# A fused attention and spectral-mix kernel: pairing other key blocks, and value products over 64 partitions

## The chip, the cores and the metric

The kernel runs on one core of a Trainium2 chip. The metric is the device time of one execution in microseconds, and the number to predict is the median of the changed kernel's runs. The kernel before takes 438.14 us (median of three runs, 438.12 to 438.55).

## The reference

The reference is a sliding-window attention whose output feeds a spectral layer. Batch, heads, sequence and head size are 8, 8, 576 and 64; a query sees itself and the 127 keys before it, with a linear bias by distance.

```python
scores = scale * np.matmul(q, k.transpose(0, 1, 3, 2))
rel = pos[:, None] - pos[None, :]
mask = (rel >= 0) & (rel < window)                  # window = 128
scores = np.where(mask, scores + bias[None], -1e9)  # bias = -slope(head) * |rel|
attn = np.exp(scores - max); attn = attn / attn.sum(-1)
x = np.matmul(attn, v)                              # 8 x 576 x 512 after the heads are joined
X = np.fft.rfft(x, axis=1)                          # the first 64 modes are kept
Yr = Xr @ w_r - Xi @ w_i ;  Yi = Xr @ w_i + Xi @ w_r   # per mode, 512 x 512 weights
u = x + np.fft.irfft(Y)
out = u + np.maximum(u @ w_ch, 0.0)
```

The weights `moe_w_r` and `moe_w_i` are 64 matrices of 512 x 512 in fp32 each, 134 MB together. They are by far the largest input; `q`, `k` and `v` are 9.4 MB each.

## The kernel before, in words

The kernel has two parts that overlap in their transfers. The **attention part** works through 16 units; a unit is one batch entry and four heads. A table `STAGE` (line 38) fixes by hand the order in which the steps of neighbouring units are issued, with a lag for each step; one pass through the table is called a stage here, and a stage finishes one unit's worth of each step. The **spectral part** streams the 128 weight matrices through TensorE (line 886) and ends with the projections and the output.

For a unit, `q` and `k` are loaded in fp32, cast to bf16 by VectorE (line 251), transposed by TensorE (line 263) and copied out by ScalarE (line 269), so that the head's 64 dimensions lie on partitions. `score` (line 274) multiplies keys by queries. The 576 tokens are four full blocks of 128 (numbers 0 to 3) and a tail of 64. A score tile holds two key blocks. A block has 128 keys, and they are taken as 64 pairs: the even keys (j = 0) and the odd keys (j = 1) of a block are the two halves of the free dimension, and the two blocks of a tile are the two halves of the partitions. So partitions 0 to 63 belong to the first block of the tile, partitions 64 to 127 to the second. In the kernel before, tile pair 0 holds blocks 0 and 1, pair 1 holds blocks 2 and 3. `exp` (line 305) runs on ScalarE; pair 0 is then multiplied by a table of decays on VectorE (`mask`, line 312), while pair 1 got its bias by a matmul with the identity (line 284) before the exponent.

`value` (line 320) multiplies the attention tile, as the stationary operand (128 partitions by 128 queries), by the values `vb`. Since the two halves of the partitions hold different key blocks, whose windows reach different query tiles, `vb` is laid out with zeros: the values of the first block fill columns 0 to 65 of its rows and zeros the rest, the values of the second block columns 66 to 131 (64 columns of values and two of ones, for the sum). One matmul of 132 columns over all 128 partitions thus serves two neighbouring query tiles. `vt` holds the tail keys. `norm` (line 352) divides by the sums on VectorE.

The values are loaded by five DMAs for each unit: one for each head, 128 partitions by two pieces of 512 bytes (line 212), and one for the tail, which writes partitions 64 to 95 (line 225). They go through the SP queue, which holds nothing else during attention but the loads of `q` and `k`. The last two units' values go through the POOL queue in three DMAs (lines 219 and 225), because their place in time is among POOL's weight loads. The cast of the values (line 246) takes two VectorE instructions of 64 partitions, one for each half, and line 248 casts the tail. After a cast, the loads for the unit after next are issued, so each kind of input has two buffers.

What sets the order of the weight loads: POOL issues them in program order. In most stages of the attention part, POOL first copies one element of the cast `k` of the unit after next (`gate`, line 565) and then issues one weight load of 512 KB (as bf16; the DMA reads 1 MB of fp32 and casts). From stage 12 on it also loads weights into the buffers of `q`, `k` and `v` that are no longer needed (line 472 with tiles `qr`, `kr`, `vr`), and then packs of two matrices into memory that the attention part gives back (line 491). POOL's own work at the start is the masks' distances (line 159) and the zeros and ones of `vb` and `vt` (lines 139 to 142).

Of the kernel before, what the change touches and what calls it, by code (L numbers as in the profile page):

```python
# [11 lines left out]
BF16 = mybir.dt.bfloat16  # L12
I32 = mybir.dt.int32
AF = mybir.ActivationFunctionType
ALU = mybir.AluOpType
# [5 lines left out]
P = 128  # L21
D = 64
# [5 lines left out]
FULL = 4  # L28
# [2 lines left out]
TPP = 9  # L31

W = D + 2

NC = 24

# [70 lines left out]
class _Attention:  # L107


    def __init__(self, tc, ctx, q, k, v, consts, x, XC, raw):  # L110
        self.tc, self.nc = tc, tc.nc
        self.q, self.k, self.v = q, k, v
        self.ident, self.F, self.FT = consts
        self.x, self.XC = x, XC
        B, H, S, _ = q.shape
        self.S, self.NG = S, H // 4
        self.units = [(b, g) for b in range(B) for g in range(self.NG)]
        self.raw = raw
        end = ctx.enter_context(tc.tile_pool(name="aend", bufs=1))
        self.sums = ctx.enter_context(tc.tile_pool(name="asum", bufs=2))  # L120
        self.mid = ctx.enter_context(tc.tile_pool(name="amid", bufs=2))
        self.ps = ctx.enter_context(tc.tile_pool(name="aps", bufs=1, space=PSUM))
        fix = ctx.enter_context(tc.tile_pool(name="afix", bufs=1))
        self.table = fix.tile([P, H, 2, 2 * P], BF16, name="mask")
        self.bias = fix.tile([P, H, 2, 2 * P], BF16, name="bias")
        self.qkT = [fix.tile([P, 2, 2, (FULL + 1) * P], BF16, name=f"qkT{i}") for i in range(2)]
        at = (fix, end)
        self.att = [at[i].tile([P, FULL * 8 * P + 64], BF16, name=f"att{i}") for i in range(2)]
        self.vb = [at[i].tile([P, 2, 4, 2, 2 * W], BF16, name=f"vb{i}") for i in range(2)]
        self.vt = [end.tile([P, 4, 2, W], BF16, name=f"vt{i}") for i in range(2)]  # L130
        self.loaded, self.casted, self.open = {}, {}, {}

    def fixtures(self, i):
        nc = self.nc
        for t, tail in ((self.vb[i], self.vt[i]),):
            for half in range(2):
                row = slice(64 * half, 64 * half + 64)
                c0 = W * half
                nc.gpsimd.memset(t[row, :, :, :, W - c0 : 2 * W - c0], 0.0)
                nc.gpsimd.memset(t[row, :, :, :, c0 + D : c0 + W], 1.0)  # L140
            nc.gpsimd.memset(tail, 0.0)
            nc.gpsimd.memset(tail[64:96, :, :, D:], 1.0)
        nc.gpsimd.memset(self.att[i][:, FULL * 8 * P :], 1.0)

    def distances(self, pool):

        nc = self.nc
        key_i = pool.tile([P, 2, 2], I32)
        for half in range(2):
            nc.gpsimd.iota(key_i[64 * half : 64 * half + 64], [[1, 2], [-P, 2]], base=0,  # L150
                           channel_multiplier=2)
        key = pool.tile([P, 2, 2], FP32)
        nc.gpsimd.tensor_copy(key, key_i)
        self.near = [pool.tile([P, 2, 2 * P], BF16) for _ in range(2)]

        def window(out, half, c0, width, n):
            row = slice(64 * half, 64 * half + 64)
            sign = 1 - 2 * n
            nc.gpsimd.affine_select(
                out=out[row, :, c0 : c0 + width],  # L160
                in_=key[row, :, n].unsqueeze(-1).broadcast_to([64, 2, width]),
                compare_op=ALU.is_ge, fill=-float(2**20), base=-n,
                pattern=[[-sign, 2], [sign, width]], channel_multiplier=-2 * sign,
            )

        for half in range(2):
            for n in range(2):
                window(self.near[0], half, n * P, P, n)
        nc.gpsimd.tensor_copy(self.near[1][:64], self.near[0][:64])
        nc.gpsimd.tensor_copy(self.near[1][64:, :, : P + TAIL], self.near[0][64:, :, : P + TAIL])  # L170
        window(self.near[1], 1, P + TAIL, TAIL, 0)

    def slope(self, h):
        return 2.0 ** (-8.0 * (h + 1) / self.table.shape[1])
# [26 lines left out]
    def load(self, w, u):  # L201
# [5 lines left out]
        if w == "v":  # L207
            t = self.raw[w][:, u % 2]
            sv = self.v[b, hs]
            if u < len(self.units) - 2:  # L210
                for h in range(4):
                    nc.sync.dma_start(
                        out=t[:, :2, h],
                        in_=sv[h, : FULL * P].rearrange("(r p j) d -> p r (j d)", r=2, j=2),
                    )
                queue = nc.sync
            else:
                for r in range(2):
                    nc.gpsimd.dma_start(
                        out=t[:, r],  # L220
                        in_=sv[:, 2 * r * P : 2 * (r + 1) * P].rearrange(
                            "h (p j) d -> p h (j d)", j=2),
                    )
                queue = nc.gpsimd
            queue.dma_start(
                out=t[64:96, 2],
                in_=sv[:, FULL * P :].rearrange("h (p j) d -> p h (j d)", j=2),
            )
        else:
            t = self.raw[w][:, u % 2]  # L230
            src = (self.q, self.k)["qk".index(w)][b, hs]
            nc.sync.dma_start(
                out=t.rearrange("p e j d -> p e (j d)"),
                in_=src.rearrange("(e h) (p j) d -> (h p) e (j d)", h=2, j=TPP),
            )
        self.loaded[w, u] = t

    def cast(self, u, w):
# [2 lines left out]
        src = self.loaded.pop((w, u))  # L241
        if w == "v":
            src = src.rearrange("p s h (j d) -> p s h j d", j=2)
            for half in range(2):
                row = slice(64 * half, 64 * half + 64)
                nc.vector.tensor_copy(  # L246
                    self.vb[u % 2][row, :, :, :, W * half : W * half + D], src[row, :2])
            nc.vector.tensor_copy(self.vt[u % 2][64:96, :, :, :D], src[64:96, 2])
        else:
            dst = self.mid.tile([P, TPP, 2, D], BF16, tag=w, name=w)  # L250
# [23 lines left out]
    def score(self, u, t):  # L274
# [12 lines left out]
                )  # L287
        for j in range(2):
            for half in range(2):
                blk = 2 * pair + half  # L290
                spans = [(blk * P, 0, min(2 * P, self.S - blk * P))]
                if blk == FULL - 1:
                    spans.append((FULL * P, 192, TAIL))
                for k0, c0, n in spans:
                    for e in range(2):
                        row = slice(64 * e, 64 * e + 64)
                        nc.tensor.matmul(  # L297
                            sc[64 * half : 64 * half + 64, e, j * 256 + c0 : j * 256 + c0 + n],
                            lhsT=qkT[row, 1, h, k0 + j : k0 + P : 2],
                            rhs=qkT[row, 0, h, k0 : k0 + n],  # L300
                            start=not biased, stop=True, skip_group_check=biased,
                        )
        self.open[t, u] = sc
# [16 lines left out]
    def value(self, u, e):  # L320
# [1 line left out]

        nc = self.nc
        b, g = self.units[u]
        odd = b % 2
        att, vb, vt = self.att[u % 2], self.vb[u % 2], self.vt[u % 2]
        last = u == len(self.units) - 1 and e == 1
        av = self.ps.tile([P, 2, 512], FP32, tag="sc" if last else "av", bufs=2 if last else 1)
        for h in range(2):
            bank = av[:, h, : (FULL + 1) * W]  # L330
            todo = []
            for pair in range(2):
                rhs = [vb[:, pair, 2 * e + h, j] for j in range(2)]
                todo.append((pair, 0, 2 * pair, rhs))
                if pair == 1 and odd:
                    todo.append((pair, P, 3, [r[:, :W] for r in rhs]))
                    todo.append((pair, P - 64, 4, [r[:, W:] for r in rhs]))
                else:
                    todo.append((pair, P, 2 * pair + 1, rhs))
            todo.append((1, 192 - 64 * odd, 4, [vt[:, 2 * e + h, j] for j in range(2)]))  # L340
            for n, (pair, c0, qt, rhs) in enumerate(todo):
                for j in range(2):
                    o = (((2 * pair + h) * 2 + e) * 2 + j) * 256 + c0
                    nc.tensor.matmul(  # L344
                        bank[:, qt * W : qt * W + rhs[j].shape[1]],
                        lhsT=att[:, o : o + P], rhs=rhs[j],
                        start=(n == 0 and j == 0), stop=(n == len(todo) - 1 and j == 1),
                        skip_group_check=True,
                    )
        self.open["av", e, u] = av  # L350

    def norm(self, u, e):
# [2 lines left out]
        av = self.open.pop(("av", e, u))  # L355
        cs = slice((4 * g + 2 * e) * D, (4 * g + 2 * e + 2) * D)
        rec = self.sums.tile([P, 2, FULL + 1], FP32, tag="rec", name="rec")
        tiles = av[:, :, : (FULL + 1) * W].rearrange("p h (t n) -> p h t n", n=W)
        nc.vector.reciprocal(rec, tiles[:, :, :, D])
        nc.vector.tensor_tensor(  # L360
            out=self.x[:, b, :, cs].rearrange("p t (h d) -> p h t d", h=2),
# [667 lines left out]
```

## Time and profile before

| | before |
|---|---|
| median of three runs | 438.14 us |
| profiled execution | 437.99 us |
| its span | 436.1 us |
| busy share of the span: PE, DVE, ACT, POOL | 73%, 42%, 37%, 21% |
| read from HBM, written | 162.5 MB, 9.4 MB |
| granted TensorE clock, mean of the span | 0.862 |

All shares and times below the first two rows are of the profiled execution. Its span is 1.89 us shorter than its time; this remainder lies around the span. A line such as `2.00:8.00` of the windows gives the busy time of each engine in that stretch, then the granted clock, the mean busy share of the 16 DMA engines (packets of one engine overlap, so it can exceed 1) and the bytes that arrived, in GB/s. Weights count there in bf16, though twice as many bytes are read.

### The profile page before, as it was taken

How to read it: one execution, taken by the hardware profiler on the slowest of the kernel's cores; microseconds unless marked ns; L12 is line 12 of the kernel's file. 1: busy time of each engine (PE TensorE's matmuls, PEld its weight loads, DVE VectorE, ACT ScalarE, POOL GpSimd, SP SyncE). 2: the span in 40 equal slices, each digit the busy share in tenths (PEclk: the TensorE clock that was granted, in tenths of full speed). 3: DMA queues.
4: the chain of work that ended last, by engine and by line, in shares of the span. 5: the costliest groups of instructions: out<-in, count | busy, mean ns of one | idle time of the engine just before them, and what ended most of it. 6: DMA issues, size and time to landing. Idle time of an engine off the chain costs nothing.

```text
span 436.1 us, 8292 instructions
## 1 busy us (share of the span) xinstructions
PE 316.2 (73%) x3488; PEld 177.7 (41%) x3509; DVE 184.5 (42%) x332; ACT 162.3 (37%) x211; POOL 90.2 (21%) x170
## 2 busy tenths in 40 slices
PE   5589899979686635543442487999889999788982
PEld 4367677757565312111111133444434444334430
DVE  7789799887783301000000021322213233122684
ACT  6949899988681000000000011322222322102780
POOL 8701010103424002222112110101111110012600
PEclk9969999999999955555555569999999999989997
DMA  8999999999999999999999999999999999998598
GB/s 285 326 311 310 290 316 300 307 298 299 252 217 212 215 215 213 214 214 214 215 212 214 214 215 214 215 214 215 215 214 214 215 215 215 213 215 153 190 378 311
DMA packets 50453, 105.54 MB, mean 242 GB/s; under 512 B 4032, under 2 KB 21072, under 8 KB 50416
## 3 DMA queue, kind: packets, MB, share of 16 engines
q0 software_dynamic: 19440, 68.41, 77.9%
q1 hardware_dynamic: 30976, 36.60, 25.3%
q8 instruction: 27, 0.44, 0.4%
q14 instruction: 10, 0.08, 0.1%
HBM read 162.53 MB, written 9.44 MB: 394 GB/s over the span
## 4 chain that ended last, share of the span: by engine, by line
DMA 71%; PE 10%; DVE 8%; issue 5%; POOL 2%; ACT 1%; SPq 1%; DVEq 0%; POOLq 0%; ACTq 0%
DMA w<-in_moe_w_i_dram 42%; DMA wch<-in_moe_w_ch_dram 8%; DMA qr<-in_q_dram 7%; DMA vr<-in_v_dram 6%; DVE o L842 3%; DMA qr<-in_moe_w_i_dram 3%; PE my L702 2%; DMA vr<-in_moe_w_r_dram 2%; DMA kr<-in_k_dram 2%; DVE vb L246 1%; PE acc L886 1%; PE av L344 1%; POOL Z L648 1%; PE my L659 1%; DVE att L318 1%
## 5 line engine op out<-in xcount | busy, mean ns | idle before, releaser
L886 PE MATMUL acc<-w,XC 128*32 128x512 bf16 x456 | 80.3, 478 | 68.5 <-DMA w<-in_moe_w_i_dram 34.2
L886 PEld LDWEIGHTS <-XC 128*32 128x32 bf16 x508 | 38.4, 147 | 109.2 <-issue 82.8
L307 ACT ACTIVATE att<-sc 128x1024 bf16<-128x1024 f32 x64 | 64.1, 1032 | 9.7 <-PE sc L297 9.6
L636 ACT CAST ZW<-zw 128x512 bf16<-128x512 f32 x8 | 4.7, 585 | 142.9 <-PE zw L634 142.9
L344 PE MATMUL av<-vb,att 128*128 128x132 bf16 (+1 forms) x576 | 38.4, 217 | 13.3 <-DVE x L360 8.6
L344 PEld LDWEIGHTS <-att 128*128 128x128 bf16 x704 | 36.6, 98 | 18.7 <-DVE x L360 12.0
L608 DVE TENSOR_SCALAR yq<-acc 128x512 bf16<-128x512 f32 x14 | 9.6, 687 | 81.8 <-PE acc L886 81.8
L702 PE MATMUL my<-wch,xT 128*64 128x512 bf16 x288 | 34.5, 381 | 5.7 <-ACT x L733 4.2
L711 ACT CAST XW<-my 128x512 bf16<-128x512 f32 x36 | 19.3, 589 | 50.5 <-PE my L659 50.5
L683 DVE COPY xT<-tr 128x1024 bf16<-128x1024 bf16 x18 | 12.4, 692 | 54.9 <-PE tr L681 54.9
L269 ACT COPY qkT<-tp 128x1152 bf16<-128x1152 bf16 x30 | 33.5, 1116 | 4.1 <-PE tp L263 3.6
L491 POOL DMA_DIRECT2D w<-in_moe_w_r_dram x22 | 15.6, 710 | 72.1 <-PE acc L886 46.1
L491 POOL DMA_DIRECT2D w<-in_moe_w_i_dram x23 | 16.3, 709 | 64.1 <-PE acc L886 45.3
L297 PE MATMUL sc<-qkT 64*64 64x256 bf16 (+2 forms) x640 | 25.1, 263 | 4.8 <-ACT qkT L269 1.2
L360 DVE TENSOR_TENSOR x<-av,rec 128x640 bf16<-128x640 f32 x32 | 26.4, 825 | 1.1
L702 PEld LDWEIGHTS <-xT 128*64 128x64 bf16 x288 | 17.1, 109 | 21.5 <-issue 9.1
L246 DVE CAST vb<-vr 64x1024 bf16<-64x1024 f32 x32 | 22.6, 708 | 0.2
L733 ACT CAST x<-my 128x512 bf16<-128x512 f32 x18 | 10.5, 585 | 31.6 <-PE my L659 31.6
L297 PEld LDWEIGHTS <-qkT 64*64 64x64 bf16 x640 | 14.5, 109 | 19.1 <-issue 16.0
L734 DVE CAST x<-my 128x512 bf16<-128x512 f32 x18 | 12.4, 692 | 21.7 <-PE my L659 21.7
L842 DVE TENSOR_TENSOR o<-yy,r 128x1024 f32<-128x1024 f32 (+1 forms) x20 | 20.3, 1059 | 2.1 <-ACT r L802 1.9
L318 DVE TENSOR_TENSOR att<-att,mask 128x1024 bf16<-128x1024 bf16 x32 | 20.5, 682 | 0.0
(137 smaller groups left out, 424.7 us busy)
## 6 DMA issues: line engine op xcount, KB each, us to landing
w<-in_moe_w_i_dram POOLq DMA_DIRECT2D x23, 1024.0 KB, 36.2
w<-in_moe_w_r_dram POOLq DMA_DIRECT2D x22, 1024.0 KB, 35.6
qr<-in_q_dram SPq DMA_DIRECT2D x16, 576.0 KB, 7.9
kr<-in_k_dram SPq DMA_DIRECT2D x16, 576.0 KB, 7.9
w<-in_moe_w_r_dram POOLq DMA_DIRECT2D x16, 512.0 KB, 14.2
vr<-in_v_dram SPq DMA_DIRECT2D x56, 128.0 KB, 7.6
w<-in_moe_w_i_dram POOLq DMA_DIRECT2D x13, 512.0 KB, 24.0
out_dram<-o SPq DMA_DIRECT2D x13, 512.0 KB, 5.0
```

The lines of the kernel that those rows point to most:

```text
L246: nc.vector.tensor_copy(self.vb[u % 2][row, :, :, :, W * half : W * half + D], src[row, :2])
L269: (self.nc.vector.tensor_copy if u < 2 and w == "q" else self.nc.scalar.copy)(dst.rearrange("q h (p j) -> q h p j", j=TPP), tp.rearrange(" ...
L297: nc.tensor.matmul(sc[64 * half : 64 * half + 64, e, j * 256 + c0 : j * 256 + c0 + n], lhsT=qkT[row, 1, h, k0 + j : k0 + P : 2], rhs=qkT[r ...
L307: self.nc.scalar.activation(self.att[u % 2][:, kt * 8 * P : (kt + 1) * 8 * P], sc.rearrange("p e n -> p (e n)"), AF.Exp, scale=1.0 / math. ...
L318: nc.vector.tensor_tensor(out=rows, in0=rows, in1=self.table[:, heads], op=ALU.mult)
L344: nc.tensor.matmul(bank[:, qt * W : qt * W + rhs[j].shape[1]], lhsT=att[:, o : o + P], rhs=rhs[j], start=(n == 0 and j == 0), stop=(n == l ...
L360: nc.vector.tensor_tensor(out=self.x[:, b, :, cs].rearrange("p t (h d) -> p h t d", h=2), in0=tiles[:, :, :, :D], in1=rec.unsqueeze(-1).br ...
L491: nc.gpsimd.dma_start(out=t.rearrange("p s a e -> p s (a e)"), in_=w[kinds.pop()][m : m + 2].rearrange("m (p a) e -> p m (a e)", a=4))
L702: nc.tensor.matmul(mm[ROWS[half]], lhsT=lhsT, rhs=wch[:, dt], start=(dt == 0), stop=False, skip_group_check=True,)
L711: nc.scalar.copy(XW[:, j, n], mms[n])
L842: nc.vector.tensor_tensor(out=o[:, c], in0=yy[:, c], in1=r[:, c], op=ALU.add)
L886: nc.tensor.matmul(into[32 * (m % 4) : 32 * (m % 4) + 32], lhsT=XC[:, c0 : c0 + 31 * NM + 1 : NM], rhs=wq[t][a], start=(ri == 0 and a == 0 ...
```

## The change

The tile pairs become blocks 1 and 2, and blocks 0 and 3 (`BLOCKS`). In pair 0, the first half's queries are tiles 1 and 2; the second half (block 2) covers query tiles 2 and 3, and its columns are placed so that query tile 2 lies in the same columns for both halves. For one of the two key parities this needs the span to be cut in two. So query tile 2 is the one that both halves of a pair share, and its product still contracts over 128 partitions. All other products take one half: 64 partitions of attention weights by 64 partitions of values, 66 columns wide. `vb` loses its zeros and is half as wide. One VectorE instruction of 128 partitions casts it. The output tile `av` is laid out by query tile in steps of `SLOT`, with both heads side by side, so query tiles 0 to 2 lie in one PSUM bank and 3 and 4 in the next. `value` issues the products of the lower half and of the upper half in turn, two heads each, and the shared tile and the tail keys at the end: 32 matmuls where there were 20 (even batch entries) or 24 (odd).

The values are still loaded by five DMAs for each unit, but the block order changes what each writes: two DMAs of two heads for blocks 1 and 2 (128 partitions), one of four heads for block 0 (partitions 0 to 63), one of four heads for block 3 (partitions 64 to 127), and the tail. Every contiguous piece is 512 bytes, as before. The last two units use the same five on the POOL queue instead of three. On POOL, the memsets of the zeros go, and the distances take more and smaller selects.

```diff
+SLOT = 172
+BLOCKS = ((1, 2), (0, 3))
...
-        self.vb = [at[i].tile([P, 2, 4, 2, 2 * W], BF16, name=f"vb{i}") for i in range(2)]
+        self.vb = [at[i].tile([P, 2, 4, 2, W], BF16, name=f"vb{i}") for i in range(2)]
...
-                nc.gpsimd.memset(t[row, :, :, :, W - c0 : 2 * W - c0], 0.0)
-                nc.gpsimd.memset(t[row, :, :, :, c0 + D : c0 + W], 1.0)
...
+        nc.gpsimd.memset(self.vb[i][:, :, :, :, D:], 1.0)
...
-            if u < len(self.units) - 2:
-                for h in range(4):
-                    nc.sync.dma_start(
-                        out=t[:, :2, h],
-                        in_=sv[h, : FULL * P].rearrange("(r p j) d -> p r (j d)", r=2, j=2),
...
-                for r in range(2):
-                    nc.gpsimd.dma_start(
-                        out=t[:, r],
...
+            queue = nc.sync if u < len(self.units) - 2 else nc.gpsimd
+            for rows, r, first in ((slice(0, P), 0, 1), (slice(0, 64), 1, 0), (slice(64, P), 1, 3)):
+                for hh in (slice(0, 2), slice(2, 4)) if r == 0 else (slice(0, 4),):
+                    n = 2 * (rows.stop - rows.start)
+                    queue.dma_start(
+                        out=t[rows, r, hh],
+                        in_=sv[hh, first * P : first * P + n].rearrange("h (p j) d -> p h (j d)", j=2),
...
-            for half in range(2):
-                row = slice(64 * half, 64 * half + 64)
-                nc.vector.tensor_copy(
-                    self.vb[u % 2][row, :, :, :, W * half : W * half + D], src[row, :2])
+            nc.vector.tensor_copy(self.vb[u % 2][:, :, :, :, :D], src[:, :2])
...
-                blk = 2 * pair + half
-                spans = [(blk * P, 0, min(2 * P, self.S - blk * P))]
-                if blk == FULL - 1:
-                    spans.append((FULL * P, 192, TAIL))
...
+                k0, c0 = BLOCKS[pair][half] * P, 2 * P * j
+                spans = [(k0, k0, c0, min(2 * P, self.S - k0))]
+                if biased and half:
+                    spans.append((FULL * P, FULL * P, c0 + 3 * TAIL, TAIL))
+                elif half and j == 0:
+                    spans = [(k0, k0, P, 2 * P)]
+                elif half:
+                    spans = [(k0, k0, 3 * P, P), (k0, k0 + P, 0, P)]
...
+        for j in range(2):
+            c0 = 2 * P * j
+            todo += [(low, 1, 0, c0, vb, j), (high, 0, 3, 2 * P - c0, vb, j),
+                     (low, 1, 1, c0 + P, vb, j), (high, 1, 3, c0, vb, j),
+                     (low, 0, 1, c0, vb, j), (high, 1, 4, c0 + P - back, vb, j)]
+            far += [(slice(0, P), 0, 2, c0 + P, vb, j), (high, 1, 4, c0 + 3 * TAIL - back, vt, j)]
+        started = set()
+        for row, pair, qt, c0, src, j in todo + far:
+            for h in range(2):
+                vals = src[row, pair, 2 * e + h, j] if src is vb else src[row, 2 * e + h, j]
+                o, d = ((2 * pair + h) * 2 + e) * 4 * P + c0, qt * SLOT + h * W
+                nc.tensor.matmul(
+                    flat[:, d : d + W], lhsT=att[row, o : o + P], rhs=vals,
+                    start=(qt > 2) not in started, stop=True, skip_group_check=True,
+                )
+                started.add(qt > 2)
```

## The prediction

> **What bounds the kernel now.** I read the profile page's slices, queues and chain first, to see which resource is full, and then windows of time, to see whether it is full in the stretch that changes.
>
> ```profile
> DMA  8999999999999999999999999999999999998598
> GB/s 285 326 311 310 290 316 300 307 298 299 252 217 212 215 215 213 214 214 214 215 212 214 214 215 214 215 214 215 215 214 214 215 215 215 213 215 153 190 378 311
> ...
> q0 software_dynamic: 19440, 68.41, 77.9%
> q1 hardware_dynamic: 30976, 36.60, 25.3%
> q8 instruction: 27, 0.44, 0.4%
> ...
> DMA 71%; PE 10%; DVE 8%; issue 5%; POOL 2%; ACT 1%; SPq 1%; DVEq 0%; POOLq 0%; ACTq 0%
> ```
>
> The DMA engines are full from the second slice to about 400 us, where the last weights land; after that the span ends by fixed steps that this change doesn't touch. The chain is 71% DMA. During attention the rate is about 300 GB/s, a mix of inputs (q1) and weights (q0), then 214 GB/s of weights alone.
>
> ```profile
> 2.00:8.00 6.00, 4.31 (x38) 3.58 (x36) 5.35 (x12) 3.15 (x5) 5.57 (x11) 1.00 0.99 369
> 8.60:10.00 1.40, 0.64 (x8) 0.19 (x8) 1.40 (x4) 0.66 (x2) 1.30 (x4) 1.00 1.20 303
> 10.20:10.60 0.40, 0.00 (x0) 0.00 (x0) 0.40 (x1) 0.40 (x1) 0.35 (x1) 1.00 1.25 252
> 10.60:11.00 0.40, 0.00 (x0) 0.00 (x0) 0.40 (x1) 0.40 (x2) 0.39 (x1) 1.00 0.99 221
> 34.00:120.00 86.00, 73.42 (x1393) 58.31 (x1398) 72.67 (x132) 75.06 (x85) 15.43 (x34) 1.00 1.07 296
> 119.00:120.00 1.00, 1.00 (x25) 0.65 (x22) 0.97 (x3) 0.45 (x1) 0.46 (x1) 1.00 0.83 225
> 240.00:280.00 40.00, 29.05 (x203) 13.05 (x200) 7.95 (x16) 5.60 (x11) 5.62 (x8) 0.78 1.06 214
> ```
>
> The last two columns are the DMA share and GB/s. In the last window, weights alone, a full set of engines reads 1.06. From 34 to 120 us it reads 1.07: attention leaves no room either. The first window is q and k at their best, 369 GB/s; the second a burst of values, 303.
>
> ```profile
> 40.89 0.53 POOL L472 DMA_DIRECT2D w<-in_moe_w_r_dram  x1 [0.27 <-issue]
> ...
> 99.38 0.53 POOL L472 DMA_DIRECT2D w<-in_moe_w_r_dram  x1 [0.27 <-issue]
> ```
>
> Between these two weight loads lie eight stages: 58.49 us, 7.31 us each. A stage moves q and k (1.18 MB), values (0.59 MB) and one weight matrix (0.52 MB). At 369, 303 and 214 GB/s that is 3.20 + 1.95 + 2.45 = 7.60 us; with q and k at the 399 GB/s of 4 to 6 us, 7.36. So the stage is as long as its transfers. Computing alone would need less: 73.42 us of PE in 86 us is 6.24 us for each 7.31, VectorE 6.18, ScalarE 6.38.
>
> **The change, part by part.**
>
> *VectorE.* Two casts of 64 partitions become one of 128:
>
> ```profile
> L246 DVE CAST vb<-vr 64x1024 bf16<-64x1024 f32 x30 | 20.5, 684 | 0.2
> L251 DVE CAST q<-qr 128x1152 bf16<-128x1152 f32 x13 | 9.9, 761 | 6.8 <-DMA qr<-in_q_dram 6.8
> ```
>
> The q cast sets the price of 128 partitions: 761 x 1024/1152 = 676 ns, so 0.69 us less for each unit, 11 us in all. On the path it is worth nothing: the next thing on VectorE is the cast of k or q, which waits for its DMA (6.8 us for q above). The loads behind a cast leave SP earlier and stand longer in a full queue.
>
> *TensorE, values.* From the chain, 20 matmuls (16 of 132 columns, 4 of 66) take 1.18 us and 24 (12 and 12) take 1.24 us. With the 0.19 us of one matmul's own length off, that is 53 ns for 132 columns and 34 for 66. Now 32 of 66: one after the other 1.09 us, against 0.99 to 1.05. If lower and upper halves run at once, as the score products on 64 partitions do (16 of 256 columns in 0.63 us), 24 of them halve: 0.68 us. So between +0.2 and -0.7 us for a unit's two groups. Each switch between half and full height may cost a drain; the bound is one 66-column matmul's mean of 195 ns less its 34, 0.16 us, three more in a group: up to 1.0 us for a unit. The score tiles gain four matmuls for a unit, of 128 columns in place of 256, at the same sum of columns: under 0.1 us. All this lies beneath 7.31 us of transfers; I take zero, and the worst case is a rival.
>
> *POOL.* At the start 4.4 us of memsets of zeros go (0.97 and 1.03 us for the first unit, 0.97 and 1.43 for the second), so the first weight load leaves earlier than 11.36 us, into engines already full: nothing. For the last two units five DMAs replace three. The 256 KB issue took 0.78 us, the 64 KB one 0.59; four of about 0.65 for two of 0.78 add 1.0 us for each unit, at 105 and 114 us. Behind them wait the gate and the weight loads into qr and kr, and POOL's queue has at most eight in flight, so the later ones now wait for pieces of values or weights issued five to eight places before. The load issued at 108.60 landed 10.9 us later: that much is queued, so 1 to 2 us of issue is hidden. The first pack into returned memory (128.91 us) now also waits for the last unit's mask, which ended at 130.2. Loads issued up to 128.4 land until 136.6, so that is hidden too.
>
> *Instruction fetch.* TensorE gets 384 more matmuls, with a weight load each. q8 fetched 0.44 MB in 27 packets for 8292 instructions; 768 more are about three packets. 0.4% of 436 us is 1.7 us for 27, so +0.2 us of DMA time.
>
> *The value loads.* Bytes, the 512-byte pieces and the count of DMAs on SP stay. But two of the five now write only 64 partitions: 262 KB for a unit, 4.19 MB in all. The only load of fewer than 128 partitions before is the tail, at the end of each burst. In the two windows that hold the first tails' end, 10.20 to 11.00, the rate fell from 303 to 252 and 221 GB/s. So 4.19 MB take 13.8 us at 303, 16.6 at 252, 19.0 at 221: the change costs 0 to 5.2 us of DMA time, and DMA time is the span. I take +2.0. It is nearer the 252 row, but below it, because that window also holds the first pieces of the next load, and because after the first stages weights fill the engines between the pieces.
>
> [...]
>
> *Sum.* 436.1 + 2.0 + 0.2 = 438.3 us of span; with the 1.89 us around it 440.2. The profiled run stood 0.15 below the median, so 440.3 us. A change under 0.2%, 0.9 us, can't be told from none here.
>
> **The rivals.**
>
> 1. *The half-height loads cost nothing.* Lower and upper pieces follow each other in a queue, and engines that are some pieces apart write to different halves. For it: tails' median landing is 7.4 us, not longer than the 7.6 of the 128-partition loads. Against: the falling windows. Time: 437.99 + 0.2 + 0.15, 438.3: no change.
> 2. *TensorE becomes the bound of a stage.* All values one after the other and every switch a full drain: 6.24 + 0.2 + 1.0 = 7.44 us for 7.31; it decides from 1.07 us more for a unit on. Over 14 stages 1.8 us on top of rival 1: 440.1; with both, 442. Against: busy time counts the overlapping length of matmuls, so the true occupation is lower.
> 3. *Faster: earlier issue fills small holes.* The share fell to 0.83 at 119 us and to between 1.01 and 1.05 in ten windows of 2 us before 60 us, against 1.06: 0.6 us by 60 us, perhaps 1.3 us over attention. If VectorE's 0.69 us brings each load to the queue sooner, these holes close: 438.1 - 1.3 + 0.2 = 437.0. It decides if the half-height cost stays under 0.2 us. Against: a share of 1.02 with 16 full engines may hold no hole at all.
> [...]
>
> [...]
>
> **How the numbers follow.** Forecast with half-height loads at +1 to +4 us, its own range 439.3 to 442.3: 0.42. Rival 4 and beyond: 0.08. Rival 2: 0.09. Rival 1: 0.27. Rival 3: 0.14. Slower is the first three, 0.59; same 0.27; faster 0.14. The range leaves out a tenth at each end: from 437.1 to 443.6.
>
> **What the profile after would show.** The share from 34 to 120 us stays near 1.07; the distance of the weight loads at line 469 grows from 7.31 by about 0.13 us if the forecast holds, stays if rival 1 holds. The first value burst falls below 303 GB/s before its tail. L251's wait for the DMA grows, since VectorE has more time. The time from the last weights to the end stays at 436.1 less 402.4 us, the last weight's matmul. I am wrong if the gates move closer, if TensorE has no idle time left between 34 and 120 us, or if the share falls under 1.

## The result and the profile after

The changed kernel takes 457.01 us (median of six runs, 453.63 to 462.12), beside 438.35 us for the kernel before on the same chip: 1.040 times as long, with an interval of 1.0325 to 1.0472. The prediction said slower, at 440.3 us with a range up to 443.6. The direction came, the size did not: 18.7 us in place of 2. The profiled execution, 462.12 us, is the longest of the six and a slow one (granted clock 0.820; the median without it is 456.1 us), so its details are stronger than the median's.

The page of the changed kernel has these lines (DMA share and rate by slice, the queues, the chain):

```profile
DMA  8999999999986999999999999999999999999498
GB/s 277 299 286 274 271 259 253 277 253 241 248 185 123 198 213 215 214 213 214 214 215 212 214 215 214 214 214 215 214 214 215 214 214 216 213 215 188 146 372 317
...
q0 software_dynamic: 19504, 68.41, 74.1%
q1 hardware_dynamic: 30976, 36.60, 28.0%
q8 instruction: 30, 0.49, 0.4%
...
DMA 68%; PE 18%; DVE 4%; issue 3%; ACT 2%; POOL 2%; SPq 2%; DVEq 0%; ACTq 0%; POOLq 0%
```

The line to read is q1, the queue of the inputs. It has the same 30976 packets and the same 36.60 MB as before. But 28.0% of a span of 460.3 us is 128.9 us of 16 engines' time, where before 25.3% of 436.1 us was 110.3. The same bytes in the same packets keep the engines busy 18.6 us longer. The weights (q0) grew by only 1.4 us, from 339.7 to 341.1, and the instruction fetch has its three packets more.

The kept traces hold each packet's size and time, and on q1 the size tells what a packet carries. Summed and divided by 16 engines, in us:

| packets of q1 | before | changed |
|---|---|---|
| 16128 of 512 bytes: the values of the 14 units on SP | 30.1 | 38.2 |
| 8192 of 2304 bytes: `q` and `k` | 53.6 | 63.6 |
| the rest: the output, and 4 bytes at the end of each transfer | 26.8 | 27.1 |

So the values' own packets took 8.1 us more, and those of `q` and `k`, whose loads didn't change, 10.0 us more. (The page's shares are rounded, hence 18.6 above.)

The windows of the changed kernel (last two columns: DMA share, GB/s) say where:

```profile
8.60:10.00 1.40, 0.64 (x10) 0.37 (x10) 1.40 (x5) 0.67 (x1) 1.34 (x4) 1.00 1.20 265
34.00:120.00 86.00, 70.92 (x1469) 51.70 (x1474) 57.84 (x103) 66.45 (x75) 7.99 (x22) 0.91 1.09 261
120.00:140.00 20.00, 11.46 (x185) 8.40 (x186) 6.58 (x12) 10.41 (x12) 6.91 (x12) 0.78 0.86 188
140.00:160.00 20.00, 16.32 (x292) 11.34 (x293) 12.23 (x23) 10.76 (x12) 5.13 (x10) 0.71 0.89 170
```

The last two windows in the kernel before:

```profile
120.00:140.00 20.00, 14.96 (x267) 12.04 (x266) 12.87 (x26) 10.67 (x14) 6.17 (x10) 1.00 1.06 215
140.00:160.00 20.00, 11.64 (x124) 6.91 (x121) 4.01 (x15) 0.00 (x0) 3.21 (x6) 0.80 1.06 214
```

From 34 to 120 us the engines are as busy as before (1.09, it was 1.07) and move less: 261 GB/s, it was 296. That is a slower transfer, not a wait. After it, from 120 to 160 us, there is a wait: the share falls to 0.86 and 0.89. Against 1.06 for full engines this is about 20 x 0.20/1.06 + 20 x 0.17/1.06 = 7 us of empty engines. 18.6 and 7 make 25.6 us, and the span grew by 24.2; some of the two lies side by side. The empty stretch is not what makes the loss: `e2` below, with a profiled time near its median, has none (1.05 and 1.06 in these two windows) and is still 16.8 us slower than the kernel before.

POOL's weight loads, eight stages apart, and the chain of the changed kernel, in order of time:

```profile
42.73 0.53 POOL L469 DMA_DIRECT2D w<-in_moe_w_r_dram  x1 [0.27 <-issue]
...
112.21 0.53 POOL L469 DMA_DIRECT2D w<-in_moe_w_r_dram  x1 [0.27 <-issue]
```

```profile
120.44 19.21 DMA kr<-in_k_dram
...
159.52 2.80 POOL w L488 x4
162.31 30.12 DMA w<-in_moe_w_r_dram
...
421.48 1.04 PE pa L883 x4
```

A stage is 69.48/8 = 8.69 us, it was 7.31. The last load of `k`, a full-height load that the change didn't touch, takes 19.2 us to land. What stands behind it (transposes, scores, values) ends at 159.5, and only then POOL may issue the rest of the weights for the memory that attention gives back; that is the empty stretch. The rest of the kernel is only shifted: before, this matmul stood at

```profile
397.41 1.04 PE pa L886 x4
```

so 24.07 us of the 24.2 are there by then. The table of issues (KB, median us from issue to landing), of the changed kernel and then of the kernel before, shows that the full-height neighbours suffer too:

```profile
qr<-in_q_dram SPq DMA_DIRECT2D x16, 576.0 KB, 11.3
kr<-in_k_dram SPq DMA_DIRECT2D x16, 576.0 KB, 9.4
vr<-in_v_dram SPq DMA_DIRECT2D x56, 128.0 KB, 9.4
```

```profile
qr<-in_q_dram SPq DMA_DIRECT2D x16, 576.0 KB, 7.9
kr<-in_k_dram SPq DMA_DIRECT2D x16, 576.0 KB, 7.9
...
vr<-in_v_dram SPq DMA_DIRECT2D x56, 128.0 KB, 7.6
```

### The profile page after: what moved, and what is told of

It reads as the page before. It is cut to its first block, busy times and chain, and to the rows that moved or that the text cites. A ratio compares the mean times of both kernels' runs of the same rounds, so it can differ in the third digit from the quotient of the medians.

```text
span 460.3 us, 9045 instructions
## 1 busy us (share of the span) xinstructions
PE 332.1 (72%) x3872; PEld 182.7 (40%) x3893; DVE 173.2 (38%) x316; ACT 162.7 (35%) x211; POOL 85.7 (19%) x170
## 3 DMA queue, kind: packets, MB, share of 16 engines
q1 hardware_dynamic: 30976, 36.60, 28.0%
## 4 chain that ended last, share of the span: by engine, by line
DMA 68%; PE 18%; DVE 4%; issue 3%; ACT 2%; POOL 2%; SPq 2%; DVEq 0%; ACTq 0%; POOLq 0%
DMA w<-in_moe_w_i_dram 34%; DMA vr<-in_v_dram 10%; DMA wch<-in_moe_w_ch_dram 8%; DMA w<-in_moe_w_r_dram 7%; DMA qr<-in_q_dram 4%; PE av L341 4%; DMA kr<-in_k_dram 4%; PE my L699 2%; PE tp L257 2%; PE sc L295 2%; PE acc L883 2%; DVE o L839 2%; PE sc L278 1%; DMA out_dram<-o 1%; PE my L656 1%
## 5 line engine op out<-in xcount | busy, mean ns | idle before, releaser
L305 ACT ACTIVATE att<-sc 128x1024 bf16<-128x1024 f32 x64 | 64.1, 1030 | 16.4 <-PE sc L295 16.4
L341 PE MATMUL av<-vb,att 64*128 64x66 bf16 (+1 forms) x896 | 34.2, 204 | 28.6 <-DVE x L357 20.2
L341 PEld LDWEIGHTS <-att 64*128 64x128 bf16 (+1 forms) x1024 | 30.9, 101 | 41.3 <-DVE x L357 13.5
L295 PE MATMUL sc<-qkT 64*64 64x256 bf16 (+3 forms) x704 | 28.3, 279 | 5.0 <-issue 2.0
L488 POOL DMA_DIRECT2D w<-in_moe_w_i_dram x23 | 16.4, 712 | 66.2 <-PE acc L883 45.1
L295 PEld LDWEIGHTS <-qkT 64*64 64x64 bf16 x704 | 18.7, 119 | 21.6 <-issue 18.3
L562 POOL COPY gate<-k 1x1 bf16<-1x1 bf16 x13 | 2.3, 178 | 95.2 <-DVE rec L356 59.3
## 6 DMA issues: line engine op xcount, KB each, us to landing
qr<-in_q_dram SPq DMA_DIRECT2D x16, 576.0 KB, 11.3
```

The costliest lines, as they stand in the source:

```text
L295: nc.tensor.matmul(sc[64 * half : 64 * half + 64, e, c0 : c0 + n], lhsT=qkT[row, 1, h, k0 + j : k0 + P : 2], rhs=qkT[row, 0, h, q0 : q0 + ...
L305: self.nc.scalar.activation(self.att[u % 2][:, kt * 8 * P : (kt + 1) * 8 * P], sc.rearrange("p e n -> p (e n)"), AF.Exp, scale=1.0 / math. ...
L341: nc.tensor.matmul(flat[:, d : d + W], lhsT=att[row, o : o + P], rhs=vals, start=(qt > 2) not in started, stop=True, skip_group_check=True,)
L488: nc.gpsimd.dma_start(out=t.rearrange("p s a e -> p s (a e)"), in_=w[kinds.pop()][m : m + 2].rearrange("m (p a) e -> p m (a e)", a=4))
```

## The experiments

For each run the "q1 time" is the share of q1 times the span, as above; 110.3 us for the kernel before and 128.9 for the changed one. Times are medians beside the kernel before on the same chip (438.6 to 439.1 us).

### Is it the loads?

`e1_full_loads`: the changed kernel, loads alone undone (it leaves out the values of blocks 0 and 3).

```diff
-            for rows, r, first in ((slice(0, P), 0, 1), (slice(0, 64), 1, 0), (slice(64, P), 1, 3)):
-                for hh in (slice(0, 2), slice(2, 4)) if r == 0 else (slice(0, 4),):
+            for rows, r, first in ((slice(0, P), 0, 1), (slice(0, P), 1, 2)):
+                for hh in (slice(0, 2), slice(2, 4)):
```

> The changed kernel, with the second pair's values loaded by two DMAs of 128 partitions in place of two of 64. Left out: blocks 0 and 3 don't reach their places; blocks 2 and 3 lie there as one contiguous piece, so bytes, piece size and the number of DMAs stay. Theory L (the loads of 64 partitions carry the whole loss): 437.5 to 439.5 us, the rate from 34 to 120 us back at 296 GB/s, no idle DMA engines about 135 us. Theory C (the value products over 64 partitions and their mode switches lengthen the stage): 450 us or more, DMA idle before the attention's end as in the changed kernel. Both in part: 443 to 450 us.

`e2_before_half_loads`: the kernel before, with half-height loads alone put in.

```diff
-                for h in range(4):
-                    nc.sync.dma_start(
-                        out=t[:, :2, h],
...
+            for rows, r, first in ((slice(0, P), 0, 0), (slice(0, 64), 1, 2), (slice(64, P), 1, 3)):
+                for hh in (slice(0, 2), slice(2, 4)) if r == 0 else (slice(0, 4),):
...
```

> The kernel before, with its blocks 2 and 3 loaded by one DMA of partitions 0 to 63 and one of partitions 64 to 127, four heads each, on SP and, for the last two units, on POOL; all else as before. Theory L: 452 to 458 us, with value packets of 45 to 50 ns in the half-height pieces seen as a rate near 265 GB/s from 34 to 120 us. Theory C: 438 to 439 us.

`e3_natural_loads`: the changed kernel with full-height loads of neighbouring blocks; four casts of 64 partitions, two of which move between the halves, then sort the blocks.

```diff
+            for rows, r, first in ((slice(0, P), 0, 0), (slice(0, P), 1, 2)):
+                for hh in (slice(0, 2), slice(2, 4)):
...
-            nc.vector.tensor_copy(self.vb[u % 2][:, :, :, :, :D], src[:, :2])
+            for pair in range(2):
+                for half in range(2):
+                    r, row = BLOCKS[pair][half] // 2, 64 * (BLOCKS[pair][half] % 2)
+                    nc.vector.tensor_copy(
+                        self.vb[u % 2][64 * half : 64 * half + 64, pair, :, :, :D],
+                        src[row : row + 64, r])
```

> The changed kernel with values loaded in the order of memory, blocks 0 and 1, then 2 and 3, by four DMAs of 128 partitions and two heads, and cast by four VectorE instructions of 64 partitions that put the blocks in their places, two of them across the halves. The output is the full one. Theory L: 437.5 to 439.5 us, since 0.9 us more of VectorE in a stage has cover: 57.8 us busy of 86 in the changed kernel. Theory C: 450 us or more. No version is expected clearly under 438 us by theory L, because the transfers set the pace.

Measured: e1 438.75 us, ratio 1.0004 (0.998 to 1.0027); e2 455.62, 1.0359 (1.03 to 1.0419); e3 439.61, 1.0013 (0.999 to 1.0035). The attention window of e1, q1 on its page, and q1 of e2:

```profile
34.00:120.00 86.00, 77.64 (x1707) 57.28 (x1710) 67.06 (x121) 76.47 (x86) 17.34 (x36) 0.98 1.07 296
```

```profile
q1 hardware_dynamic: 30976, 36.60, 25.3%
```

```profile
q1 hardware_dynamic: 30976, 36.60, 28.2%
```

With full-height loads all the new matmuls, casts and selects cost nothing and gain nothing: 1.07 and 296 GB/s again, q1 time 110.6 us of a span of 437.3. Without them, the loads alone give the loss: q1 time 127.7 us of 453.0. Split by packet size as above, e1 has 30.4 us of values and 53.3 of `q` and `k`, e2 37.7 and 62.9. The price is taken here as the changed kernel less e1, 457.0 - 438.75 = 18.3 us; e2, on the kernel before, gives 16.8, and the interval of the changed kernel's ratio leaves 14 to 21.

### Is it a price for each load?

`e8_half_of_units` and `e10_two_sides_12` take the half-height loads in 8 and in 12 of the 16 units, and full-height ones in the others. Below is e8; e10's condition is `2 <= u < len(self.units) - 2`.

```diff
+            pieces = [(slice(0, P), 0, 1, slice(0, 2)), (slice(0, P), 0, 1, slice(2, 4))]
+            if u % 4 < 2 and u < len(self.units) - 2:
+                pieces += [(slice(0, 64), 1, 0, slice(0, 4)), (slice(64, P), 1, 3, slice(0, 4))]
+            else:
+                pieces += [(slice(0, P), 1, 2, slice(0, 2)), (slice(0, P), 1, 2, slice(2, 4))]
...
```

> The changed kernel with half-height loads in units 0, 1, 4, 5, 8, 9, 12, 13 alone; the others load at full height (blocks 2 and 3 in place of 0 and 3, so values wrong there). If each half-height load has its own price: half of 18.7 us, 447 to 448.5 us. If the price grows because engines fall apart over many stages in a row, so that full-height stages between let them catch up: 440 to 446 us. Over 450 would say that a few such loads already disturb the stages behind them.

> The control for one side: the changed kernel with half-height loads, one piece for each half, in the third to the fourteenth unit, and full-height loads (blocks 2 and 3 in place of 0 and 3) in the other four. With 1.13 us for a unit, as 8 units gave 9.0 us: 12 units 13.5 us, 452.6 us. Under 449 or over 456 would say that the price for a unit isn't fixed.

Measured: 448.16 us beside 439.14, ratio 1.0203 (1.0182 to 1.0224), and 453.1 beside 438.78, 1.0306 (1.0245 to 1.0367). So 8 units cost 9.0 us, 12 units 14.3 and 16 units 18.3: 1.13, 1.19 and 1.14 us for a unit. The intervals are wide (8.0 to 9.8, 10.8 to 16.1 and 14.2 to 20.7 us), but within them the price goes with the number of such loads; engines that fall apart more and more are not needed for it. The q1 time is 26.5% of 447.0, 118.5 us, in e8, and 28.0% of 452.4, 126.7, in e10: 8.2 and 16.4 us more than before, less even for a unit than the time is.

### Is it the side or the height?

`e6_one_side` was meant to put both pieces on partitions 0 to 63 (shown against e10):

```diff
-                pieces += [(slice(0, 64), 1, 0, slice(0, 4)), (slice(64, P), 1, 3, slice(0, 4))]
+                pieces += [(slice(0, 64), 1, 0, slice(0, 4)), (slice(0, 64), 1, 3, slice(0, 4))]
```

> The changed kernel, where from the third unit to the fourteenth both 64-partition pieces are written to partitions 0-63 (the upper half keeps older data, so blocks 0 and 3 get wrong values), and the other four units load at full height. 12 of 16 units keep the half-height transfers, so if the price lies in the height of a transfer alone, and pieces for different halves never help each other: three quarters of 18.7 us, 452 us. If the pieces for the two halves do overlap a little in the changed kernel and one half's way into the memory is what is short, taking the overlap away costs more: 456 to 475 us. Under 447 would speak against both.

It took 476.42 us, ratio 1.0849 (1.0822 to 1.0877), and tells nothing of sides. Both pieces write one place, so the second was held on SP until the first had landed, as its table of SP's waits shows (us in total, times, longest):

```profile
SPq L222 <- DMA vr<-in_v_dram: 68.8, 12, 8.9
```

Its packets do tell something: with one half-height piece under way at a time and the engines no longer full (a share of 0.87 from 34 to 120 us), the value packets took 30.7 us, where the kernel before has 30.1 and e10, with the same 12 units, 37.3.

`e9_one_side_apart` sends the second piece to rows 0 to 63 of the tail's slot, `(slice(0, 64), 2, 3, slice(0, 4))`.

> The kernel of e6 had both pieces written to one place, so SP held the second piece back until the first had landed (68.8 us of waits of SP on value loads, 12 times), and its 476 us say nothing of sides. Here, from the third unit to the fourteenth, both 64-partition pieces again go to partitions 0-63, but to two places (the tail's slot takes the second), so nothing waits; blocks 0 and 3 get wrong values. Theory H (only the height counts): as the next kernel, which has the same units with one piece for each half, 452.6 by 1.13 us for each of 12 units. Theory S (each half has its own way in, and pieces for different halves that are under way together help each other): 455 to 462 us, more than the next kernel by 2 us or more.

Measured: 456.5 us (453.12 to 460.43), ratio 1.0369 (1.0286 to 1.0452), beside 453.1 and 1.0306 of its control e10. The median is where theory S had it, 3.4 us above the control, but the four runs spread over 7 us, the intervals overlap, and the q1 time speaks the other way: 27.6% of 451.3 is 124.6 us, below the control's 126.7. One side or two makes no difference that these runs can tell, as long as the pieces follow each other in one queue.

`e13_upper_on_act` lets the two halves be under way at once: ScalarE's queue issues the upper piece of 12 units. `e14_full_on_act` is its control, where that queue issues one full-height load.

```diff
-                    queue.dma_start(
+                    (nc.scalar if rows.start and 2 <= u < len(self.units) - 2 else queue).dma_start(
```

> The changed kernel with its whole output, but in the third to the fourteenth unit the piece for partitions 64-127 is issued by ScalarE's queue, so that pieces for both halves can be under way at once at their full size. Theory S (a half's transfers are slow because they have only one half's way in, and both halves together fill it): 439 to 447 us, and the share of q1 times the span falls from 129 to under 118 us. Theory H (a packet into a half-height load is slow whatever runs beside it): 452 to 460 us, with 124 us or more.

> The control for ScalarE's queue: full-height loads (blocks 2 and 3 in place of 0 and 3, so values wrong there), one of the four value loads of the third to the fourteenth unit issued by ScalarE. 438 to 441 us if the issue on ScalarE costs little (12 issues by about 0.6 us, with 0.9 us of ScalarE free in a stage of 7.31); over 443 would say that what the kernel with upper pieces on ScalarE loses is partly ScalarE's waiting.

Measured: e13 451.69 us, ratio 1.0303 (1.0269 to 1.0337); e14 443.19, 1.011 (1.0068 to 1.0152). The queues of e13 and of e14 (q10 is ScalarE's):

```profile
q1 hardware_dynamic: 27712, 35.03, 25.5%
q10 hardware_dynamic: 3264, 1.57, 1.6%
```

```profile
q1 hardware_dynamic: 27712, 35.03, 23.6%
q10 hardware_dynamic: 3264, 1.57, 1.2%
```

Both queues together are 27.1% of 449.4, 121.8 us, against 24.8% of 441.3, 109.4 us. That is 12.4 us of extra packet time where the changed kernel has 18.3 over e1, so a third went, though four of the 16 units kept their pieces in one queue; in time, 8.5 us are left of 18.3. Most of what went is in `q` and `k` (58.6 us, 63.6 in the changed kernel); the value packets of both queues still take 36.3 us (38.2, and 30.5 in the control). Neither theory's figures hold: side by side the halves help each other in part, and the height costs on. The control itself lost 4.6 us (its DMA share from 34 to 120 us is 1.02), so the difference of the two isn't clean.

### Can smaller pieces in turn repair it?

`e4_alternate_halves` cuts each half-height load in four of one head (32 KB), `e7_two_head_pieces` in two of two heads (64 KB), lower and upper in turn. Below is e7; e4 has four such pieces for each half.

```diff
...
+            for hh in (slice(0, 2), slice(2, 4)):
+                pieces += [(slice(0, 64), 1, 0, hh), (slice(64, P), 1, 3, hh)]
...
```

> The changed kernel with the two half-height loads of a unit on SP cut into eight of one head each, lower and upper half in turn (32 KB each); the last two units as in the changed kernel. If the loss comes from all engines writing one half at a time, engines that are a few pieces apart now write to different halves, and much of it goes: 440 to 447 us. If any DMA of 64 partitions is slow by itself, or if the engines stay in step: 452 to 460 us.

> The changed kernel with its whole output; each 64-partition load is cut in two of two heads (64 KB), lower and upper half in turn: seven value loads and two others to issue for a unit, nine by about 0.7 us, 6.3 us, less than the 7.31 us of a stage. The kernel with pieces of one head took 474 us, but there SP issued 13 loads for a unit back to back, 9.1 us for a unit, and loads landed after 5 to 6 us in place of 9 to 11. If that was all issue time and the alternation does relieve the transfers: 439 to 447 us. If alternation relieves nothing: about 457 us, as the changed kernel.

Measured: e4 474.03 us, ratio 1.0815 (1.0783 to 1.0846), a miss; e7 458.46, 1.0431 (1.0405 to 1.0456), as the changed kernel. SP's timeline in e4:

```profile
64.25 7.38 SPq L224 DMA_DIRECT2D vr<-in_v_dram  x10
71.72 0.53 SPq L228 DMA_DIRECT2D vr<-in_v_dram  x1
72.35 0.38 SPq L235 DMA_DIRECT2D kr<-in_k_dram  x1
72.82 0.42 SPq L235 DMA_DIRECT2D qr<-in_q_dram  x1
```

Thirteen loads take 9.0 us with no pause between them, so SP's issuing has become the bound of the stage, and its queue runs low: the q1 time is only 23.8% of 472.7, 112.5 us, near the 110.3 of before, and loads of `q` land after 5.8 us. The packets are no longer slow (30.3 us of values, 54.6 of `q` and `k`) and the engines are no longer full (a share of 0.90 from 34 to 120 us). e7 stands between, 25.0% of 456.5, 114.1 us, with a share of

```profile
34.00:120.00 86.00, 72.74 (x1447) 52.98 (x1450) 56.09 (x100) 65.27 (x74) 8.66 (x22) 0.86 1.01 258
```

It moves 258 GB/s with emptier engines. What these two save in packet time they lose in gaps. So smaller pieces are no cure; whether they would be one with cheaper issues stays open.

### Can one load write both blocks at full height?

`e5_joined_blocks`: blocks 0 and 3 of a head in one transfer of 128 partitions.

```diff
...
+            for h in range(4):
+                queue.dma_start(
+                    out=t[:, 1, h],
+                    in_=sv[h, : FULL * P].rearrange("(b p j) d -> b p (j d)", b=FULL, j=2)[::3],
+                )
```

> The changed kernel with its own layout and its whole output, but blocks 0 and 3 of a head arrive by one 128-partition transfer (block 0 into partitions 0-63, block 3 into 64-127), four such transfers for a unit in place of two of 64 partitions; SP issues seven value loads for a unit in place of five. Theory H (transfers that write only 64 partitions are the whole loss): 438 to 440 us, as with the full-height loads whose values were left out (438.75). Theory I (what was saved there came from leaving values out or from the order of the pieces): over 445 us.

Measured: 529.48 us, ratio 1.2054 (1.2036 to 1.2072), an entire miss, for a reason of its own: by its time theory I would hold, but e3, with the whole output at 439.61 us, speaks against that. The queues of e5, and of e7, which issues as many input loads:

```profile
q1 hardware_dynamic: 30640, 36.60, 21.4%
```

```profile
q1 hardware_dynamic: 31424, 36.60, 25.0%
```

Same bytes, 784 packets fewer. e7 issues two loads for a unit more than the changed kernel and has 31424 - 30976 = 448 packets more, 14 units times 2 times 16: a load closes with 16 small packets. In e5 784 are missing, 56 joined loads times 14, so each of these closed with two. Two is also the number of blocks, the outermost loop of the source, and e11's count below agrees with its outermost loop in the same way. The engines' mean share from 34 to 120 us is only 0.66. Loads carried by two engines in place of sixteen would fit this, but the traces name no engine for a packet, so it is not shown.

### Does the kernel before pay for its tails?

The tail loads of the kernel before write 32 partitions. `e11_wide_tails` and `e12_even_wide_tails` write the same 64 KB to 128 partitions by 512 bytes, and the cast takes one head's part for all. In e11 the source is the tail rows with the four heads outermost (`"h (p j) d -> h p (j d)"`); in e12, below, it is one even block.

```diff
-                out=t[64:96, 2],
-                in_=sv[:, FULL * P :].rearrange("h (p j) d -> p h (j d)", j=2),
+                out=t[:, 2, 0],
+                in_=sv[0, : 2 * P].rearrange("(p j) d -> p (j d)", j=2),
...
-            nc.vector.tensor_copy(self.vt[u % 2][64:96, :, :, :D], src[64:96, 2])
+            nc.vector.tensor_copy(
+                self.vt[u % 2][64:96, :, :, :D],
+                src[64:96, 2, 0].unsqueeze(1).broadcast_to([32, 4, 2, D]))
```

> The kernel before, with its one load of low height changed: the tail's 64 KB go to 128 partitions by 512 bytes in place of 32 partitions by 2 KB, same bytes, same packets; the cast of the tail then takes one head's part for all four, so the tail's values are wrong. If 32-partition loads pay the price of the 64-partition ones (1.13 us for 262 KB, 0.28 us for 64 KB, 14 units on SP): 4 us or more faster, 431 to 435 us. If a single short load among full ones is hidden: 438 to 439.5 us.

> e11 was 12 us slower, but its tail transfers closed with four completion packets in place of 16 (168 fewer for 14 transfers), so four engines moved each. Here the tail's 64 KB are read as one even block of another place of the values (256 rows of one head), 128 partitions by 512 bytes, so all engines share it; the tail's values are wrong. q1 should count 30976 packets again. If the kernel before pays for its 32-partition tails as the changed one pays for 64 partitions (1.15 us for 262 KB): 14 times 0.29 us less, 434 to 435.5 us. If one short load among full ones costs nothing: 438 to 439.5 us.

Measured: e11 450.83 us, ratio 1.0241 (1.0169 to 1.0313), a miss; e12 436.49, 0.9948 (0.9927 to 0.9968). q1 of e11, then of e12:

```profile
q1 hardware_dynamic: 30808, 36.60, 24.8%
```

```profile
q1 hardware_dynamic: 30976, 36.60, 24.6%
```

e11 lacks 168 packets, 14 loads times 12: four closing packets for four heads, the outermost loop of its source (that four engines moved each is again a reading of this count). One load of 64 KB for a unit that closes with four packets in place of 16 costs 12 us in all (7 to 14 by the interval). e12, evenly spread, is 2.1 us faster than before, and its q1 time is 24.6% of 434.3, 106.8 us, 3.5 less. So the kernel before seems to pay for its low loads, less than expected: 0.15 us for a unit's 64 KB, and most of it in the packets of `q` and `k` (3.1 us less, the values 0.5). The height is not all that changed, though: e12 also reads one contiguous piece where the tails are four. e12 computes wrong tails, and no version with right ones was tried: the products want the tail's keys of every head on the same 32 partitions. No version that computes the whole output beat the kernel before.

## Why the prediction was wrong

*The value loads, +2.0 us.* This is the step that failed, as a size: it was priced at 0 to 5.2 us and measured 18.3 (16.8 in e2). Three things were wrong in it. First, the rows: the windows at 10.20 to 11.00 us hold a short tail among full loads, and the tail turned out cheaper for its bytes than the new loads (0.15 us for 64 KB in e12, 1.14 for 262 KB). Second, the "worst" row was taken for an upper bound, though no row of before had a half-height load of 128 KB in a full queue; the value packets alone took 8.1 us more. Third, only the bytes that change shape were priced. The larger part, 10.0 us, is in the packets of `q` and `k`, for which the sum had nothing: their loads didn't change, but stand in the same queue, and land after 11.3 and 9.4 us in place of 7.9. By what means the half-height loads slow their neighbours is not shown. With both pieces in one queue, one side (e9, 456.5 us) and two sides (e10, 453.1) can't be told apart; with two queues, e13 lost a third of the extra packet time (12.4 us in place of 18.3), mostly on `q` and `k`, against a control that was slower itself.

*The stage as long as its transfers.* Right, and the reason why the loss shows in full: 1.38 us for a stage in the profiled run. The knock-on at the end of attention, 7 us of empty engines behind one load of `k` in the profiled run, was in no step; e2 shows that the loss comes without it too. The prediction had counted a full queue as a cover for POOL's work, and did not ask what happens to the weights when the last inputs land late.

*VectorE.* Right: one cast of 128 partitions takes 685 ns,

```profile
L241 DVE CAST vb<-vr 128x1024 bf16<-128x1024 f32 x16 | 11.0, 685 | 3.9 <-DMA vr<-in_v_dram 3.8
```

and 0.69 us less for a unit is worth nothing; e1 equals the kernel before within 0.3%. The wait for `q`'s transfer grew, as said, from 6.8 us to 15.8, but for the loads' sake.

*TensorE, and rival 2.* Right to take zero. In the changed kernel's trace a group of 32 matmuls takes 1.21 us at a full clock (1.00 from 37.9 to 39.2 us). Less the 0.19 us of one matmul that is 1.02, where the prediction had 0.68 for halves that run at once and 1.09 for one after the other, plus drains. The starts in the trace tell the two apart: the first 24, of half height, start within 0.35 us, 15 ns each, less than half of the 34 ns of before; at each of the four changes between half and full height that follow, the next start comes 0.12 to 0.13 us later, where two products of one height stand 0.04 apart at most. That fits halves that run at once, and the changes of height took back what it gained, at a little less than the 0.16 us of the bound. None of it reaches the time: e1 has all of these groups and is 0.04% slower than before; rival 2 falls.

*POOL, mask, instruction fetch.* Hidden: e1 and e3 contain them all. The fetch has its three packets more, and its 0.2 us can't be told.

*Rival 1, no cost.* Its argument, that tails land no later than full-height loads (7.4 us beside 7.6), was true and proved nothing: landing is the time in a shared queue, and e12 shows that the tails cost 2.1 us all the same. *Rival 3, faster:* e1 is the test without the half-height price, and 1.0004 (0.998 to 1.0027) does not reach the 0.3% it named (437.0 us for 438.3). *A higher price of the loads, 0.08:* the right load, again too small; even the 5.2 us by the 221 GB/s row priced only the bytes that change shape.

*What the profile was to show.* The share stayed full (1.09), the first burst fell below 303 (265), the rest of the kernel was only shifted. The distance of the weight loads grew by 1.38 us where 0.13 was named; that line alone would have given the answer. None of the three signs of being wrong came: the gates moved apart, TensorE kept idle time (70.92 us busy of 86), and the share rose. They were signs of the other rivals, and none stood for a larger price of the loads.

## What to carry to other kernels

Before changing which partitions a transfer writes in a kernel whose DMA engines are full, price the transfers first: here 4.19 MB written 64 partitions at a time cost 18.3 us, more than all the vector work that the change saves (11 us), and more than half of the extra packet time fell on untouched loads in the same queue. Read a queue's share times the span, with its packets and bytes: here the same packets in more time meant slower transfers (128.9 us of q1 time, it was 110.3), 784 and 168 closing packets fewer went with sources of two and four outermost rows, and a falling share went with issues (0.90 in e4) or waits (0.87 in e6). A bound from "the nearest row" holds only if that row had the same shape in the same load; otherwise one small experiment on the old kernel (e2) tells it outright.

## What the runs showed that was not expected

- Half-height loads in a full queue cost 1.13 to 1.19 us of the kernel's time for each 262 KB, with 8, 12 or 16 such units, and about as much on one side of the partitions as on both. In the packets, more than half of it falls on the full-height loads of `q` and `k` in the same queue (10.0 us, the values 8.1).
- With the queue kept from filling by SP's issues (e4) or by a wait (e6), half-height bytes show almost no extra value-packet time (30.3 and 30.7 us against 30.1). That speaks for contention in a full queue, and not for a fixed price of the packet; it was not tested by itself, since e4 also changes the size of the pieces and both leave engines empty.
- Transfers whose source has two or four outermost rows closed with two or four packets in place of 16 (784 and 168 missing). 14 such loads of 64 KB with four rows cost 12 us, 56 with two rows 90 us.
